# The sum of two quarters in the second product: made by an accumulating DMA that GpSimd issues instead of a VectorE addition

## The chip, the cores and the metric

The kernel runs on one core of one Trainium2 chip. The metric is the device time of one execution in microseconds (us), lower is better. The core has five engines that run side by side and wait for each other through semaphores: TensorE (PE, matrix products), VectorE (DVE), ScalarE (ACT), GpSimd (POOL) and SyncE (SP, which here only issues transfers), and 16 DMA engines that carry out the transfers.

## The reference

A banded attention (each query sees itself and the 63 keys before it) over 8 batches, 8 heads, 576 positions and head size 64 gives a matrix of 4608 tokens by 512 features. Two dense layers follow, with a leaky slope of its own for each hidden feature between them:

```
attn = softmax(mask(q @ k.T / 8)) @ v          # per batch and head, window 64
x = attn as (4608, 512)
h = x @ w_in                                    # (4608, 2048)
g = maximum(h, 0) + alpha * minimum(h, 0)       # alpha: one value per hidden feature
out = g @ w_out                                 # (4608, 512)
```

All data are fp32.

## The kernel before

**What is computed where.** The 4608 tokens are cut into nine blocks of 512 tokens (`n` from 0 to 8). The first product, with the attention ahead of it, takes some 490 us; its results `g` are stored to HBM in quarters of 128 by 512 values (`hidden`, line L840). The second product, `second(n)`, then reads them back. Each block is taken in four steps of hidden features, so that there are 36 **units**, `u = 4 n + d`. A unit is one step of a Strassen-Winograd scheme: the block's `g` is split in four quarters A11, A12, A21 and A22 (tiles `g_0`, `g_1`, `g_2`, `g_3` of one set; the numbers after them are instance numbers), four sums and differences of them are formed, and seven products instead of eight are made.

**The work of a unit**, in names of the program and lines of the profile:

- `gf`: four transfers bring the quarters from HBM into the set of the unit (SP queue, L927). There are four sets (`SETS`), so a set is used again four units later.
- `z3`: `diff = A11 - A21`; `z1`: `A21 = A21 + A22`, written over A21; `z2`: `A11 = A21 - A11`, with the new A21; `z4`: `A12 = A12 - A11`. All four are VectorE instructions on 128 by 512 values (L934). `z1` can't overwrite A21 before `z3` has read it, and `z2` needs the result of `z1`.
- `parts`, seven times: the values that a product needs are split in a high part `yh` (a cast on ScalarE, L939) and a rest `yl` (a subtraction on VectorE, L940). Such a pair is called a form here. The pairs lie in a ring of ten slots; a slot is filled again when TensorE has used it.
- `O.u.i`: the product of a form, twelve matmuls (L967: `wh,yh`, `wl,yh`, `wh,yl`).
- After the fourth unit of a block the accumulated banks are put together (one copy on ScalarE, L984, seven additions on VectorE, L975) and stored (L981).

GpSimd has no part in this stage but the end of the conversion of the weights of the second product (`wh`, `wl`, L393 a cast and L390 a subtraction), which it shares with ScalarE.

**What sets the order.** Every piece of work is an `Op` with its engine, a planned duration and what it reads and writes. `Program.order` plays the whole program through with these planned durations before the kernel is built, and so fixes the order of the instructions of every engine. On the chip each engine runs its instructions in this order: where one must wait, all behind it on that engine wait too. For a transfer the planner counts the issue (`0.5`), a `service` time on the DMA engines and a landing time:

```
self.done = min(busy + LAGS[e] for e, (busy, _) in ways.items()) + (service + LANDING if service else 0.0)
```

Of the kernel before, what the change touches and what calls it, by code (L numbers as in the profile page):

```python
# [14 lines left out]
ALU = mybir.AluOpType  # L15
# [236 lines left out]
def banded_attention_then_prelu_ffn(  # L252
# [11 lines left out]
    nc = tc.nc  # L264
# [76 lines left out]
    def halves_of(*bs):  # L341
        return [f"bank.{b}.{i}" for b in bs for i in range(2)]
# [3 lines left out]
    def add(name, engine, busy, emit, *args, **kw):  # L346
        p.add(name, {engine: (busy, emit)}, *args, **kw)
# [52 lines left out]
    def w_keys_of(x, slot, halves=range(2)):  # L400
        return [f"w{x}.{slot}.{i}" for i in halves]

    raw_at = [0]

    def chunk(name, c, f, second, start=0.0):
        r = raw_at[0] % (2 if second else RAWS)
        ulps, k_ulps = ulp_ring[raw_at[0] % 2], f"e.ulps.{raw_at[0] % 2}"
# [187 lines left out]
    def value(t, i, by=V_BANK):  # L595
        av = [bank_of(b).rearrange("p (i a) q -> p i a q", i=2)[:, i] for b in by]
        pt, at = turned[t % 2].rearrange("p a h u b q -> p a h (u b q)"), 2 * (t % KRING)
        for a in range(2):
            for block, to, from_ in ((1, slice(0, P), slice(W, 3 * W)), (0, slice(0, W), slice(0, W)),
                                     (2, slice(W, P), slice(3 * W, 4 * W))):  # L600
                for h in range(2):
                    for x in range(2):
                        r, hs = slice(x * W, (x + 1) * W), slice(h * D, (h + 1) * D)
                        nc.tensor.matmul(av[x][hs, a, to], vring[r, a, at + block, hs], pt[r, a, h, from_],  # L604
                                         start=block == 1, stop=block == 2)
# [162 lines left out]
    def begin_of(n, f=0):  # L768
        return BEGIN + (CELL * min(n, N0) + CELL2 * max(n - N0, 0)) * NF + (CELL if n < N0 else CELL2) * f
# [97 lines left out]
    def new_slot():  # L867

        at = ring["at"]
        ring["at"] += 1  # L870
        return at % SLOTS, SHIFTS[at]

    def y_of(kept, x, shift):
        return kept[x][:, 16 * shift:16 * shift + 512] if 4 <= x < 8 else kept[x]

    def slot_of_form(k):

        d, at = divmod(k, 7)
        return (3 * d, 3 * d + 1, 3 * d + 2, KEPT + 2 * d, KEPT + 2 * d + 1, KEPT + 2 * d + 8, KEPT + 2 * d + 9)[at]
# [34 lines left out]
    def y_keys(x):  # L914
        return [f"yh.{x}"], [f"yl.{x}"]

    def second(n):
# [4 lines left out]
        for d in range(DUOS):  # L922
            u = n * DUOS + d
            s = u % SETS
            base = begin_of(NB) + 4.0 + u * UNIT
            for q in range(4):
                add(f"gf.{u}.{q}", "SP", 0.5, lambda s=s, q=q, d=d: nc.sync.dma_start(g_of[s][q].rearrange("p (j t) -> p j t", j=2), hidden[n][d][:, q]),  # L927
                    ["left" if s else "right", *(f"far.g.{n}.{d}.{q}.{j}" for j in range(2))], [f"g.{s}.{q}"], service=0.9, earliest=base - 45)

            def cell(q, s=s):  # L930
                return lambda: g_of[s][q]

            def both(name, to, a, b, op, reads, writes):
                add(name, "DVE", 0.61, lambda: nc.vector.tensor_tensor(out=to(), in0=a(), in1=b(), op=op), reads, writes, paired=True)  # L934

            def parts(i, value, ks):
                x, (hi, lo) = slot_of[u, i] = new_slot()
                his, los = y_keys(x)
                add(f"ys.{u}.{i}.h", "ACT", 0.54, lambda: nc.scalar.copy(y_of(y_hi, x, hi), value()), [*ks, "right"], his)  # L939
                add(f"ys.{u}.{i}.l", "DVE", 0.61, lambda: nc.vector.tensor_tensor(out=y_of(y_lo, x, lo), in0=value(), in1=y_of(y_hi, x, hi).bitcast(F32), op=ALU.subtract),  # L940
                    [*ks, *his], los, paired=True)

            a11, a12, a21, a22 = (cell(q) for q in range(4))
            k11, k12, k21, k22 = ([f"g.{s}.{q}"] for q in range(4))
            d_ = lambda: diffs[0]
            parts(1, a11, k11)
            parts(2, a12, k12)
            both(f"z3.{u}", d_, a11, a21, ALU.subtract, [*k11, *k21], ["diff"])
            both(f"z1.{u}", a21, a21, a22, ALU.add, k22, k21)
            both(f"z2.{u}", a11, a21, a11, ALU.subtract, k21, k11)  # L950
            parts(6, a11, k11)
            parts(7, d_, ["diff"])
            parts(5, a21, k21)
            both(f"z4.{u}", a12, a12, a11, ALU.subtract, k11, k12)
            parts(3, a12, k12)
            parts(4, a22, k22)
            for at, i in enumerate(ORDER):
                (x, (hi, lo)), bank = slot_of[u, i], acc[i]

                k = 7 * d + at  # L960

                def emit(k=slot_of_form(k), x=x, bank=bank, d=d, hi=hi, lo=lo):
                    done = 0
                    for part, w in ((y_of(y_hi, x, hi), w_hi), (y_of(y_hi, x, hi), w_lo), (y_of(y_lo, x, lo), w_hi)):
                        for j in range(2):
                            for h in range(2):
                                nc.tensor.matmul(banks[bank][:, h * EH:(h + 1) * EH], part[:, j * HW + h * P:j * HW + (h + 1) * P],  # L967
                                                 w[k][:, j * EH:(j + 1) * EH], start=d == 0 and not done,
                                                 stop=d == DUOS - 1 and done == 11, skip_group_check=True)
                                done += 1  # L970

                add(f"O.{u}.{i}", "PE", STEP, emit, [*w_keys_of("h", slot_of_form(k)), *w_keys_of("l", slot_of_form(k)), *y_keys(x)[0], *y_keys(x)[1]], halves_of(bank), key=base + at * STEP)
# [70 lines left out]
    for n in range(NB):  # L1043
        second(n)
# [49 lines left out]
```

## Time and profile before

| | |
|---|---|
| median of 3 runs | 835.05 us |
| the 3 runs | 833.03 to 836.2 us |
| the profiled execution, its own time | 834.97 us |
| its span, first to last instruction | 833.2 us |
| busy: PE, DVE, ACT, POOL | 821.7, 704.3, 517.6, 386.7 us |
| granted TensorE clock, mean over the span | 1.000 of full speed |

The span is what the trace covers; the profiled execution's own time is 1.8 us longer. A busy TensorE is one with a matmul in it. The view by windows gives the same busy times for a stretch, the timeline gives single instructions with the idle time of the engine before them and what ended it.

### The profile page before, as it was taken

What the parts mean: (1) busy time and instruction counts of PE and PEld (TensorE: products, weight loads), DVE (VectorE), ACT (ScalarE), POOL (GpSimd) and SP (SyncE); (2) the same over time, 40 slices, a digit from 0 to 9 for tenths busy, and PEclk for the clock granted to TensorE, in tenths of its full rate; (3) what the DMA queues carried; (4) which work ended last, traced back from release to release, by engine and by line L of the source; (5) the groups of instructions that cost most, each with busy time, mean ns of one, the idle gap of its engine ahead of it and who ended that gap; (6) DMA issues with size and microseconds to landing.
All of it is one profiled execution on the core that took longest, in us unless ns stands there. A gap on an engine that the chain in (4) does not pass through costs nothing.

```text
span 833.2 us, 23747 instructions
## 1 busy us (share of the span) xinstructions
PE 821.7 (99%) x8974; PEld 791.4 (95%) x8974; DVE 704.3 (85%) x1821; ACT 517.6 (62%) x1382; POOL 386.7 (46%) x368
## 2 busy tenths in 40 slices
PE   9999999999999999999999999999999999999998
PEld 8988888999999999999999999999999999999997
DVE  4889798999998999989865868998888897979883
ACT  6887756788776687786965666444444444444441
POOL 5899999998276471948656977000000000000000
PEclk9999999999999999999999999999999999999999
DMA  8886455546557655777555896545353544535301
GB/s 253 274 254 220 148 172 159 165 145 217 188 177 241 211 197 174 247 262 236 185 212 168 285 297 241 175 140 177 100 174 121 156 124 139 165 103 172 95 26 51
DMA packets 108882, 150.97 MB, mean 181 GB/s; under 512 B 10464, under 2 KB 69856, under 8 KB 108768
## 3 DMA queue, kind: packets, MB, share of 16 engines
q1 hardware_dynamic: 106416, 149.19, 55.4%
q8 instruction: 70, 1.15, 0.6%
q10 hardware_dynamic: 2352, 0.27, 0.2%
q14 instruction: 44, 0.36, 0.1%
HBM read 94.90 MB, written 54.53 MB: 179 GB/s over the span
## 4 chain that ended last, share of the span: by engine, by line
PE 53%; DVE 4%; ACT 1%; issue 1%; DMA 1%; POOL 1%; SPq 0%; POOLq 0%; DVEq 0%; ACTq 0%
PE bank L967 41%; PE bank L823 11%; DVE cell L838 1%; DVE bank L844 1%; DVE w L557 1%; DMA q<-qT 1%; DVE pt L583 1%; ACT cell L837 1%; PE bank L588 0%; PE bank L604 0%; ACT w L564 0%; DVE pt L581 0%; PE bank L548 0%; DMA wo<-delta 0%; ACT r L851 0%
## 5 line engine op out<-in xcount | busy, mean ns | idle before, releaser
L939 ACT CAST yh<-g 128x512 fp32r<-128x512 f32 x216 | 132.8, 622 | 128.9 <-PE bank L967 85.6
L940 DVE TENSOR_TENSOR yl<-g,yh 128x512 fp32r<-128x512 f32 x216 | 149.3, 699 | 22.1 <-ACT yh L939 21.2
L967 PE MATMUL bank<-wh,yl 128*128 128x256 f32 x1008 | 155.8, 277 | 0.0
L967 PE MATMUL bank<-wl,yh 128*128 128x256 f32 x1008 | 155.8, 277 | 0.0
L967 PE MATMUL bank<-wh,yh 128*128 128x256 f32 x1008 | 155.7, 276 | 0.0
L967 PEld LDWEIGHTS bank<-wh,yh 128*128 128x128 f32 x1008 | 133.4, 188 | 0.0
L967 PEld LDWEIGHTS bank<-wl,yh 128*128 128x128 f32 x1008 | 133.3, 188 | 0.0
L967 PEld LDWEIGHTS bank<-wh,yl 128*128 128x128 f32 x1008 | 133.3, 188 | 0.0
L564 ACT ACTIVATE w<-w,nm 128x128 f32<-128x128 f32 x288 | 112.9, 398 | 26.0 <-DVE nm L557 26.0
L823 PE MATMUL bank<-xh,wh 128*128 128x256 f32 x560 | 113.1, 283 | 4.1 <-DVE bank L844 3.5
L838 DVE SCALAR_TENSOR_TENSOR cell<-bank,alphas,cell 128x256 f32<-128x256 f32 x224 | 96.1, 477 | 21.8 <-ACT cell L837 20.1
L837 ACT ACTIVATE cell<-bank,alphas 128x256 f32<-128x256 f32 x224 | 91.8, 476 | 35.1 <-PE bank L823 19.4
L573 POOL TENSOR_TENSOR w<-w,rc 128x512 f32<-128x512 f32 x72 | 76.9, 1086 | 78.5 <-DVE rc L569 30.7
L823 PE MATMUL bank<-xh,wl 128*128 128x256 f32 x560 | 109.7, 277 | 0.0
L823 PE MATMUL bank<-xl,wh 128*128 128x256 f32 x560 | 109.5, 277 | 0.0
L823 PEld LDWEIGHTS bank<-xh,wh 128*128 128x128 f32 x560 | 84.6, 188 | 8.3 <-DVE bank L844 4.9
L823 PEld LDWEIGHTS bank<-xh,wl 128*128 128x128 f32 x560 | 84.7, 188 | 0.0
L823 PEld LDWEIGHTS bank<-xl,wh 128*128 128x128 f32 x560 | 84.7, 188 | 0.0
L934 DVE TENSOR_TENSOR g<-g,g 128x512 f32<-128x512 f32 x108 | 75.6, 700 | 1.4
L557 DVE CUSTOM_DVE_ANT_0 w<-bank,masks 128x128 f32<-128x128 f32 x288 | 64.6, 284 | 10.2 <-PE bank L548 9.9
L844 DVE TENSOR_TENSOR bank<-bank,r 128x512 f32<-128x512 f32 x84 | 58.1, 692 | 17.2 <-PE bank L823 10.7
L564 ACT ACTIVATION_READ_ACCUMULATOR w<-w,nm 128x1 f32 x288 | 56.1, 195 | 0.0
(98 smaller groups left out, 1493.6 us busy)
## 6 DMA issues: line engine op xcount, KB each, us to landing
g<-g SPq DMA_DIRECT2D x144, 256.0 KB, 4.1
g<-cell SPq DMA_DIRECT2D x141, 256.0 KB, 3.3
out<-cell SPq DMA_DIRECT2D x36, 256.0 KB, 2.3
q<-qT SPq DMA_DIRECT2D x35, 256.0 KB, 4.9
raw<-w_out SPq DMA_DIRECT2D x16, 512.0 KB, 5.2
wl<-wo SPq DMA_DIRECT2D x28, 256.0 KB, 4.6
v<-vN SPq DMA_DIRECT2D x18, 384.0 KB, 5.4
k<-kT SPq DMA_DIRECT2D x17, 384.0 KB, 4.9
```

Of the source, the lines that this page charges most:

```text
L557: nc.vector.tensor_tensor_reduce(out=of_head(weights[t % 2], g), in0=bank_of(score_banks(t, g // NP)[x])[:, e].rearrange("p (b k) -> p b k ...
L564: nc.scalar.activation(w, w, AF.Exp, scale=-1.0, bias=least[t % 2][:, g:g + 1], accum_out=sums[:, t % 2, g, 0:1])
L573: nc.gpsimd.tensor_tensor(out=w, in0=w, in1=rc.unsqueeze(1).unsqueeze(3).broadcast_to(list(w.shape)), op=ALU.mult)
L583: nc.vector.transpose(to[:, :, j ^ 1], w[:, x, j, :, j ^ 1])
L823: nc.tensor.matmul(h, at_place(w, place)[:, c * P:(c + 1) * P], v[:, c], start=new and j == 0 and not done, stop=j == 1 and done == 5, ski ...
L837: add(f"sl.{n}.{d}.{m}.{x}.{j}", "ACT", 0.36, lambda h=h, g=g, f=f: nc.scalar.activation(g, h, AF.Copy, scale=slope[:, f:f + 1]), ["signs" ...
L838: add(f"la.{n}.{d}.{m}.{x}.{j}", "DVE", 0.43, lambda h=h, g=g, f=f: nc.vector.scalar_tensor_tensor(out=g, in0=h, scalar=sign[:, f:f + 1], ...
L844: add(f"{name}.{n}.{d}", "DVE", 0.6, lambda: nc.vector.tensor_tensor(out=to, in0=a, in1=b, op=ALU.add), reads, k_to)
L934: add(name, "DVE", 0.61, lambda: nc.vector.tensor_tensor(out=to(), in0=a(), in1=b(), op=op), reads, writes, paired=True)
L939: add(f"ys.{u}.{i}.h", "ACT", 0.54, lambda: nc.scalar.copy(y_of(y_hi, x, hi), value()), [*ks, "right"], his)
L940: add(f"ys.{u}.{i}.l", "DVE", 0.61, lambda: nc.vector.tensor_tensor(out=y_of(y_lo, x, lo), in0=value(), in1=y_of(y_hi, x, hi).bitcast(F32) ...
L967: nc.tensor.matmul(banks[bank][:, h * EH:(h + 1) * EH], part[:, j * HW + h * P:j * HW + (h + 1) * P], w[k][:, j * EH:(j + 1) * EH], start= ...
```

## The change

One line of `second`: the VectorE addition `z1` becomes a transfer from A22 to A21 within SBUF that adds what it brings to what lies there. It is issued by GpSimd and planned with 0.5 us of GpSimd, a service of 1.8 us and the landing time.

```
             parts(1, a11, k11)
             parts(2, a12, k12)
             both(f"z3.{u}", d_, a11, a21, ALU.subtract, [*k11, *k21], ["diff"])
-            both(f"z1.{u}", a21, a21, a22, ALU.add, k22, k21)
+            add(f"z1.{u}", "POOL", 0.5, lambda a21=a21, a22=a22: nc.gpsimd.dma_start(a21(), a22(), accum_op=ALU.add), k22, k21, service=1.8)
             both(f"z2.{u}", a11, a21, a11, ALU.subtract, k21, k11)
             parts(6, a11, k11)
             parts(7, d_, ["diff"])
```

Since the planner plays the program anew, the order of other instructions moves too, from about the last block of the first product on. Three places follow.

**VectorE, a unit in the middle of the second product** (unit 14; `diff` is z3, the row that writes `g_0` is z2, the one that writes `g_1` is z4, each `yl` is the rest of a form). Before:

```order
L934 TENSOR_TENSOR diff<-g_0_7380,g_2_7382 128x512
L940 TENSOR_TENSOR yl_6683<-g_1_7377,yh_6682 128x512
L934 TENSOR_TENSOR g_2_7382<-g_2_7382,g_3_7383 128x512
L940 TENSOR_TENSOR yl_6685<-g_3_7379,yh_6684 128x512
L975 TENSOR_TENSOR cell_124<-bank_169,r_7388 128x512
L940 TENSOR_TENSOR yl_6688<-g_0_7380,yh_6687 128x512
L934 TENSOR_TENSOR g_0_7380<-g_2_7382,g_0_7380 128x512
L940 TENSOR_TENSOR yl_6690<-g_1_7381,yh_6689 128x512
L934 TENSOR_TENSOR g_1_7381<-g_1_7381,g_0_7380 128x512
```

And of the changed kernel, the same unit:

```order
L934 TENSOR_TENSOR diff<-g_0_7377,g_2_7379 128x512
L940 TENSOR_TENSOR yl_6683<-g_1_7374,yh_6682 128x512
L940 TENSOR_TENSOR yl_6685<-g_3_7376,yh_6684 128x512
L940 TENSOR_TENSOR yl_6688<-g_0_7377,yh_6687 128x512
L940 TENSOR_TENSOR yl_6690<-g_1_7378,yh_6689 128x512
L934 TENSOR_TENSOR g_0_7377<-g_2_7379,g_0_7377 128x512
L934 TENSOR_TENSOR g_1_7378<-g_1_7378,g_0_7377 128x512
L940 TENSOR_TENSOR yl_6672<-diff,yh_6671 128x512
L940 TENSOR_TENSOR yl_6670<-g_0_7377,yh_6669 128x512
```

The addition into `g_2` is gone, and four `yl` stand between z3 and z2, which now waits for the transfer. Counted in the same way, the instructions between z3 and z2 are 10 to 16 in units 0 to 9, 5 and 4 in units 10 and 11, and from unit 12 on 4, 8, 4 and 5 in every round of four units.

**VectorE, where the second product has just begun to run alone** (units 1 to 3: their `diff` rows, and what is behind them, to the first z2). Before, the first nine instructions:

```order
L940 TENSOR_TENSOR yl_6685<-g_0_7376,yh_6684 128x512
L934 TENSOR_TENSOR diff<-g_0_7376,g_2_7378 128x512
L934 TENSOR_TENSOR g_2_7378<-g_2_7378,g_3_7379 128x512
L940 TENSOR_TENSOR yl_6676<-g_3_7379,yh_6675 128x512
L934 TENSOR_TENSOR g_0_7376<-g_2_7378,g_0_7376 128x512
L940 TENSOR_TENSOR yl_6688<-g_1_7377,yh_6687 128x512
L940 TENSOR_TENSOR yl_6670<-diff,yh_6669 128x512
L940 TENSOR_TENSOR yl_6690<-g_0_7376,yh_6689 128x512
L934 TENSOR_TENSOR g_1_7377<-g_1_7377,g_0_7376 128x512
```

Of the changed kernel:

```order
L934 TENSOR_TENSOR diff<-g_0_7373,g_2_7375 128x512
L940 TENSOR_TENSOR yl_6676<-g_3_7376,yh_6675 128x512
L940 TENSOR_TENSOR yl_6670<-diff,yh_6669 128x512
L940 TENSOR_TENSOR yl_6688<-g_1_7374,yh_6687 128x512
L940 TENSOR_TENSOR yl_6679<-g_0_7377,yh_6678 128x512
L934 TENSOR_TENSOR diff<-g_0_7377,g_2_7379 128x512
L940 TENSOR_TENSOR yl_6685<-diff,yh_6684 128x512
L940 TENSOR_TENSOR yl_6681<-g_1_7378,yh_6680 128x512
L940 TENSOR_TENSOR yl_6670<-g_3_7380,yh_6669 128x512
L934 TENSOR_TENSOR diff<-g_0_7381,g_2_7383 128x512
L940 TENSOR_TENSOR yl_6679<-diff,yh_6678 128x512
L934 TENSOR_TENSOR g_0_7373<-g_2_7375,g_0_7373 128x512
```

Forms that need no `z1` (of units 1, 2 and 3) are drawn ahead, so that ten instructions stand between z3 and z2 of unit 1. TensorE's products are drawn ahead in the same way.

**GpSimd, the end of the weights' conversion.** Before, the last instructions of its program are these:

```order
L390 TENSOR_TENSOR wl_100<-wl_100,wh_72 128x512
L393 CAST wh_73<-wl_101 128x512
L390 TENSOR_TENSOR wl_101<-wl_101,wh_73 128x512
L390 TENSOR_TENSOR wl_102<-wl_102,wh_74 128x512
L390 TENSOR_TENSOR wl_117<-wl_117,wh_89 128x512
L390 TENSOR_TENSOR wl_118<-wl_118,wh_90 128x512
```

Of the changed kernel:

```order
L390 TENSOR_TENSOR wl_100<-wl_100,wh_72 128x512
L949 DMA g_2_7375<-g_3_7376 128x512
L949 DMA g_2_7379<-g_3_7380 128x512
L949 DMA g_2_7383<-g_3_7384 128x512
L393 CAST wh_73<-wl_101 128x512
L390 TENSOR_TENSOR wl_101<-wl_101,wh_73 128x512
L390 TENSOR_TENSOR wl_102<-wl_102,wh_74 128x512
```

The issues of the transfers of units 1, 2 and 3 stand ahead of the last four pieces of weights; that of unit 0 stands further ahead, behind the first one; those of units 4 to 35 follow at the end with nothing between them.

## Rows read from the trace of the kernel before

**Rows 1.** Page: busy us of each engine (share of the span) and instructions.

```profile
PE 821.7 (99%) x8974; PEld 791.4 (95%) x8974; DVE 704.3 (85%) x1821; ACT 517.6 (62%) x1382; POOL 386.7 (46%) x368
```

**Rows 2.** Windows: from:to, length, busy us (instructions) by engine, clock, DMA share, GB/s.

```profile
440.00:460.00 20.00, 19.10 (x165) 18.70 (x164) 13.06 (x26) 12.16 (x27) 13.71 (x12) 1.00 0.58 194
460.00:489.00 29.00, 29.00 (x250) 28.83 (x249) 21.43 (x37) 20.60 (x45) 28.92 (x23) 1.00 0.87 279
489.00:829.00 340.00, 340.00 (x2991) 339.93 (x2989) 286.42 (x451) 158.09 (x262) 21.38 (x10) 1.00 0.45 140
```

**Rows 3.** Chain that ended last, in order of time: start, us, what.

```profile
489.30 339.84 PE bank L967 x2988
829.16 0.69 DVE cell L975
```

**Rows 4.** Timeline of TensorE: start, us, operation, count [idle before <-releaser].

```profile
451.36 0.51 PE L823 MATMUL bank<-sh,wh 128*128 128x256 f32 x2 [0.85 <-DVE bank L844]
...
497.14 0.63 PE L967 MATMUL bank<-wh,yl 128*128 128x256 f32 x4
```

**Rows 5.** Timeline of VectorE, 456 to 516 us.

```profile
456.28 0.68 DVE L934 TENSOR_TENSOR diff<-g,g 128x512 f32<-128x512 f32 x1
...
458.26 0.68 DVE L934 TENSOR_TENSOR g<-g,g 128x512 f32<-128x512 f32 x1
...
493.77 1.78 DVE L934 TENSOR_TENSOR diff<-g,g 128x512 f32<-128x512 f32 x1
495.58 0.69 DVE L934 TENSOR_TENSOR g<-g,g 128x512 f32<-128x512 f32 x1
496.19 0.68 DVE L940 TENSOR_TENSOR yl<-g,yh 128x512 fp32r<-128x512 f32 x1
...
505.23 2.48 DVE L940 TENSOR_TENSOR yl<-g,yh 128x512 fp32r<-128x512 f32 x4
...
510.05 0.68 DVE L934 TENSOR_TENSOR g<-g,g 128x512 f32<-128x512 f32 x1
514.00 1.63 DVE L940 TENSOR_TENSOR yl<-diff,yh 128x512 fp32r<-128x512 f32 x1 [3.27 <-ACT yh L939]
```

**Rows 6.** Timeline of ScalarE, one cast of the second product.

```profile
620.68 0.62 ACT L939 CAST yh<-diff 128x512 fp32r<-128x512 f32 x1 [0.75 <-PE bank L967]
```

**Rows 7.** Timeline of VectorE, 621 to 623 us.

```profile
621.34 0.69 DVE L940 TENSOR_TENSOR yl<-diff,yh 128x512 fp32r<-128x512 f32 x1 [0.67 <-ACT yh L939]
622.06 0.69 DVE L934 TENSOR_TENSOR diff<-g,g 128x512 f32<-128x512 f32 x1
```

**Rows 8.** Timeline of GpSimd, 453 to 516 us.

```profile
453.05 1.29 POOL L390 TENSOR_TENSOR wl<-wl,wh 128x512 fp32r<-128x512 f32 x1
458.16 1.25 POOL L393 CAST wh<-wl 128x512 fp32r<-128x512 f32 x1 [3.83 <-DMA wl<-wo]
...
461.85 0.61 POOL L393 CAST wh<-wl 128x512 fp32r<-128x512 f32 x1
...
488.20 6.80 POOL L390 TENSOR_TENSOR wl<-wl,wh 128x512 fp32r<-128x512 f32 x5
501.33 9.87 POOL L393 CAST wh<-wl 128x512 fp32r<-128x512 f32 x1 [6.33 <-DMA wl<-wo]
511.28 5.51 POOL L390 TENSOR_TENSOR wl<-wl,wh 128x512 fp32r<-128x512 f32 x4
```

**Rows 9.** DMA issues, 520 to 820 us: count, KB each, median us to landing.

```profile
g<-g SPq DMA_DIRECT2D x113, 256.0 KB, 3.8
out<-cell SPq DMA_DIRECT2D x32, 256.0 KB, 2.4
```

**Rows 10.** Page: the queue with most bytes (packets, MB, share of 16 engines), two larger transfers.

```profile
q1 hardware_dynamic: 106416, 149.19, 55.4%
...
raw<-w_out SPq DMA_DIRECT2D x16, 512.0 KB, 5.2
...
stage<-w_in SPq DMA_DIRECT2D x5, 512.0 KB, 5.9
```

More of the change, by code (lines that the diff above doesn't have):

```diff
@@ L948, in second @@
             both(f"z3.{u}", d_, a11, a21, ALU.subtract, [*k11, *k21], ["diff"])
-            both(f"z1.{u}", a21, a21, a22, ALU.add, k22, k21)
+            add(f"z1.{u}", "POOL", 0.5, lambda a21=a21, a22=a22: nc.gpsimd.dma_start(a21(), a22(), accum_op=ALU.add), k22, k21, service=1.8)
             both(f"z2.{u}", a11, a21, a11, ALU.subtract, k21, k11)
```

## The prediction

> **What bounds the kernel now.** I read the busy time of each engine first, then windows, then the chain that ended last, then timelines. The page gives TensorE 821.7 us of a span of 833.2 [rows 1]. The windows say where that matters: from 460 to 829 us TensorE is busy without a gap [rows 2], and the chain ends with one piece of 339.84 us in which TensorE waits for nobody, behind which only one VectorE addition and a store are left [rows 3]. So in the second product TensorE alone sets the time. One matmul there takes 339.84 / 2988 = 0.1137 us, a form of twelve 1.365, a unit of seven forms 9.55, a round of four units (one block) 38.2.
>
> VectorE is the one to watch all the same: 286.42 of 340 us are busy [rows 2]. Its instructions of 128 by 512 can follow each other every (2.48 - 0.68) / 3 = 0.60 us [rows 5]. A round has 4 x 11 of them (four sums, seven rests) and 7 additions at its end: 51, or 30.6 of 38.2 us.
>
> How far VectorE is ahead decides what a delay costs. The cast at 620.68 began when TensorE freed a slot of the ring [rows 6], and its rest was done at 622.03 [rows 7]. Nine other forms are used before that slot's turn comes, 9 x 1.365 = 12.3 us after it was freed, so the form was complete 10.9 us before its use. At the start of the stage this lead isn't there yet: the rest written at 496.19 ended at 496.87 and the matmul that reads it began at 497.14, 0.27 us later [rows 4, 5]. From 496 to 511 us VectorE works without a pause, builds up the lead, and has its first idle time of 3.27 us at 514 [rows 5].
>
> **What the change removes.** 36 instructions of 0.60 us, 21.7 us of VectorE. That is worth nothing on the path, since TensorE has no gap from 460 us on. Its last idle time ahead of that is 0.85 us at 451.36 [rows 4], and the first instruction that goes is the addition at 458.26, behind it [rows 5]. Gain: 0. What it gives is spare time: a round of VectorE falls to 47 instructions, 28.2 us, and 10.0 us of the round are free.
>
> **What it adds.** A transfer of 256 KB per unit, on which z2 waits. No row shows an accumulating transfer or one issued by GpSimd, so I bound the time L from the end of z3 to the moment when z2 may start. For the issue on GpSimd: between its shortest and its usual work on 128 by 512 values, 0.61 and 1.29 us [rows 8]. For issue to landing of plain 256 KB: 2.4 us for stores, 3.8 for loads in the same stretch [rows 9]. For the second thing to be read, the old A21: the busiest queue moved 149.19 MB in 55.4% of the span [rows 10], 323 GB/s, so 0.8 us for another 256 KB. The sum is 3.8 to 5.9 us. I take the middle, 4.9, since nothing draws it to either end. The outer bounds are 2.4 (a store, and nothing for issue and addition) and 1.29 + 5.9 = 7.2, with the slowest 512 KB load [rows 10].
>
> *In a steady round* (units 12 to 35, six rounds) 4, 8, 4 and 5 instructions stand between z3 and z2. If VectorE is behind, they take 0.60 us each, and since an instruction ends 0.08 us after the next has begun, its wait per unit is L + 0.08 - 0.60 x (instructions between). Over a round that is 4 L - 12.3 us. At 4.9 it is 7.3 us, less than the 10.0 that are free: the lead stays, TensorE sees nothing. Break-even is L = 5.6. Beyond it a round loses 4 L - 22.3 us; six rounds first eat the lead of 10.9 us, and the rest is lost time. So 0.5% (4.2 us) is lost at L = 6.2, and 28 us at the bound of 7.2. What is late then: z2 holds up all rests behind it on VectorE, and TensorE waits for them.
>
> *At the start* (units 1 to 3) the thin place gets better: without the addition at 495.58 the rest used at 497.14 is done 0.6 us sooner. z3 of unit 1 ended at 495.55 [rows 5] and GpSimd is free at 495.0 [rows 8], so the first transfer lands at about 500.5. z2 of unit 1 has ten instructions ahead of it, and one of them, the rest of unit 2's A22, needs a slot that TensorE frees two forms after the one ending at about 497.6 [rows 4], at 500.3. With its cast and rest behind that (1.35 us as in rows 6 and 7) and three more instructions, z2 starts at about 503, 2.5 us after the landing. The transfers of units 2 and 3 begin at about 498 and 502 and have ten and twelve instructions too. Cost: 0. Units 4 to 9 have 11 to 16 instructions, 6.6 us at least, and units 10 and 11 sit on a lead already built.
>
> *On GpSimd's queue* the issue of unit 0 falls behind z3 at 456.28 [rows 5], into the 3.83 us in which GpSimd waited for weights [rows 8]. Those of units 1 to 3 stand ahead of the last four weight pieces, so the cast that began at 501.33 can't begin before z3 of unit 3, at about 503. Its weights are then some 2 us later than before. I count 0, since TensorE didn't wait for them, and keep the case as a rival. From there on GpSimd has only these issues, one per 9.55 us. SP's queue loses and gains nothing; the new 256 KB per unit meet DMA engines that are 45% busy [rows 2].
>
> **Sum.** 834.97 us for the profiled execution (span 833.2 and 1.8 around it), less 0, plus 0: **835.0 us**. The execution stands 0.1 us below the median of the three runs, 835.05; these lie 0.4% apart, so about 0.5%, 4 us, is what a measurement of this kernel can tell from no change.
>
> **A rule that speaks against the change.** In these rows GpSimd can be shut out: the cast of 128 by 512 that takes 0.61 us at 461.85 took 9.87 us from 501.33 [rows 8], exactly while VectorE ran additions and subtractions of two SBUF inputs without a pause, and it ended at 511.20, half a us after VectorE stopped [rows 5]. The Trainium skill (SBUF — State Buffer, section "SBUF: two separate sides") says that a transfer issued by GpSimd has its descriptors written by GpSimd's cores, and that these are shut out while VectorE holds the port pair that both share. By that the sum would be the second rival's 882 us. The same page (section "Who interferes with whom") says that a VectorE instruction with two SBUF inputs shuts out only what reads SBUF on GpSimd, while writing descriptors needs the write side. By that the sum stays 835.0. The cast reads SBUF, so the row agrees with both, and no row here shows a descriptor being written.
>
> **The rivals.**
> 1. *The transfer lands late* (slower). Place: z2 of units 12 to 35. It decides from L = 6.2 us. Price as above: 846 us at 6.5, 863 at 7.2. For it: loads in this stretch come in groups of up to four, with a median of 3.8 us against 2.4 for the stores between them [rows 9], and nothing says how fast the addition runs. Against it: even 5.9, all three terms at their upper ends but the large load, isn't enough.
> 2. *GpSimd is shut out while VectorE works*, as its cast was, so that L only starts when VectorE has stopped at z2 (slower). Then every z2 waits the full 4.9: 19.6 us a round against 10.0, 9.6 x 6 - 10.9 = 47 us, so 882. Against it: with a full lead VectorE pauses before most rests, 0.67 us at 621.34 [rows 7], and lets GpSimd in.
> 3. *The queue of GpSimd holds up the last weights* (slower). The cast starts 2 us late, and if the issues ahead of it are shut out like the cast was, up to 9.9 us. Price 2 to 10 us: about 840.
> 4. *VectorE's relief shows after all* (faster). All idle time of TensorE from 440 us on to the end of its work is 0.9 us [rows 2], so 834.1 at best, which would pass for no change. To be faster by 4 us, matmuls would have to get shorter, for which no row speaks.
>
> **How the numbers follow.** No change, transfer hidden: 0.63, own range 832 to 839 (the spread of the runs). Rival 1: 0.22, rival 2: 0.07, rival 3: 0.05, faster for a reason I don't see: 0.03. The range from 832 to 863 us takes in rival 3 and rival 1 up to its bound and leaves out the shut-out queue, landings over 7.2 us and the gain, together some 0.15. Faster by over 0.5%: 0.03, within 0.5%: 0.63, slower: 0.34.
>
> **What will show it.** Right: TensorE without a gap from about 460 us to its end, VectorE some 22 us less busy, 36 issues on GpSimd, idle time of VectorE ahead of z2 with the transfer as releaser, at most some 2 us a time, and rests still about 10 us ahead of their matmuls at the end. Wrong: waits of 3 us and more at most z2, a lead that shrinks from round to round, TensorE waiting for `yl`; or TensorE waiting for `wh` or `wl` near 515 us; or time lost before 460 us, where the order has moved too and I count nothing.

## The result and the profile after

The changed kernel takes 840.64 us (median of 18 runs, lowest 835.38) against 834.94 for the kernel before: a ratio of 1.0059, 95% interval 1.0037 to 1.0081. It is slower by a little over half a per cent, where no change was forecast. Two of the 18 runs, at 909.54 and 1166.59 us, were run at a granted clock of 0.85 and 0.66 and are left out of the ratio.

The profiled execution (836.51 us, span 834.8) is one of the faster ones. First the page's busy times, then windows (columns as in [rows 2]):

```profile
PE 822.4 (99%) x8974; PEld 792.0 (95%) x8974; DVE 678.5 (81%) x1785; ACT 506.8 (61%) x1385; POOL 406.0 (49%) x401
```

```profile
440.00:460.00 20.00, 19.14 (x168) 18.95 (x167) 13.49 (x26) 12.70 (x29) 13.21 (x12) 1.00 0.63 213
460.00:489.00 29.00, 28.79 (x244) 28.39 (x244) 19.55 (x36) 20.30 (x45) 24.09 (x19) 1.00 0.84 272
489.00:520.00 31.00, 29.75 (x254) 29.55 (x254) 26.80 (x32) 18.64 (x35) 16.99 (x14) 1.00 0.90 280
520.00:829.00 309.00, 309.00 (x2726) 309.00 (x2725) 236.52 (x384) 127.23 (x230) 27.83 (x32) 1.00 0.58 156
```

VectorE is 25.8 us less busy [rows 1] and has 36 instructions fewer. TensorE, without a gap from 460 us in [rows 2], now stands still for 0.21 us before 489 and 1.25 us before 520. The last piece of the chain that ended last starts at 498.23, not at 489.30 [rows 3]:

```profile
498.23 332.26 PE bank L967 x2920
830.51 0.69 DVE cell L975
```

What ends that gap is a rest of VectorE (the `yl` of a form). The timeline of the changed kernel around it (start, length, engine and operation, in brackets the idle time ahead of it and what ended that):

```profile
490.44 7.19 POOL L390 TENSOR_TENSOR wl<-wl,wh 128x512 fp32r<-128x512 f32 x5 [1.30 <-ACT wh L393]
...
492.99 1.80 DVE L940 TENSOR_TENSOR yl<-g,yh 128x512 fp32r<-128x512 f32 x1 [2.23 <-ACT yh L939]
...
494.72 1.77 DVE L934 TENSOR_TENSOR diff<-g,g 128x512 f32<-128x512 f32 x1
496.41 1.76 DVE L940 TENSOR_TENSOR yl<-g,yh 128x512 fp32r<-128x512 f32 x1
...
498.23 0.74 PE L967 MATMUL bank<-wh,yl 128*128 128x256 f32 x4 [1.25 <-DVE yl L940]
```

GpSimd waits 1.30 us for a weight cast of ScalarE and works on its splits until 497.63; before, it was done at 495.0 [rows 8]. Beside it these three VectorE instructions take 1.76 to 1.80 us; such an instruction alone takes 0.68. Before, one of the instructions ahead of this rest was slow, and the rest ended at 496.87 [rows 5]; now three are, and it ends at 498.17. The addition that was removed from just this place had cost 0.60. Set against the kernel before, matmul by matmul, 1.5 us are lost with this gap. Some 0.7 us were lost ahead of it, between 467 and 486 us, where the gap of 0.21 us (at 468.73, behind a VectorE instruction of the first product) lies; what brought about this part is not settled.

The transfers, from the line that issues them (ns, min/median/max; then us from issue to landing), and, of the stretch from 610 to 763 us, four rounds, VectorE's waits in the changed kernel, those in the kernel before, and the window of the changed kernel:

```profile
L949 POOL DMA_DIRECT2D g<-g x36: 862/870/1019, 456.3 to 813.0; - x36
...
DMA to landing us min/median/max: 3.3/4.8/8.2
```

```profile
DVE g L934 <- DMA g<-g: 37.5, 12, 4.1
```

```profile
DVE yl L940 <- ACT yh L939: 21.2, 28, 1.6
```

```profile
610.00:763.00 153.00, 153.00 (x1352) 153.00 (x1352) 114.81 (x187) 62.52 (x116) 13.90 (x16) 1.00 0.59 158
```

In the kernel before, VectorE waited in this stretch 21.2 us, only for casts of ScalarE: it was ahead, and held back by free slots. Now it waits 37.5 us at z2, three times a round, and for nothing else. With the 114.81 us in which it is busy that makes 152.3 of 153 us: VectorE has no time to spare. One unit of it:

```profile
649.33 0.69 DVE L934 TENSOR_TENSOR diff<-g,g 128x512 f32<-128x512 f32 x1
649.93 2.50 DVE L940 TENSOR_TENSOR yl<-g,yh 128x512 fp32r<-128x512 f32 x4
650.66 0.89 POOL L949 DMA_DIRECT2D g<-g  x1 [8.15 <-DVE yl L940]
656.28 1.42 DVE L934 TENSOR_TENSOR g<-g,g 128x512 f32<-128x512 f32 x2 [3.86 <-DMA g<-g]
```

z3 ends at 650.02, the issue starts 0.64 us later, and z2 at 656.28, 0.09 us after the landing at 656.19: up to the landing L was 6.2 here.

**Where the time goes, execution by execution.** All kernels here have the same 8,974 matmuls, so the start of matmul 5,601 (at 443 us in the kernel before), of 6,401 (537 us) and of the last (829 us) can be set against that kernel's own. This splits the difference into three: ahead of 443 us, where executions differ by some 1 us either way and in one by 3; from there to 537 us, the *start* of the second product; and behind it, the *steady* part. Worked out in this way from each trace (us), beside the runs:

| kernel | profiled | to 443 | start | steady | median (runs) | ratio, 95% interval |
|---|---|---|---|---|---|---|
| changed | 836.51 | -1.0 | +2.4 | 0.0 | 840.64 (18) | 1.0059 [1.0037, 1.0081] |
| after_again | 840.33 | -0.1 | +2.4 | +2.9 | 841.80 (6) | 1.0074 [1.0046, 1.0102] |
| after_third | 842.54 | +1.0 | +2.1 | +4.3 | one run | |
| after_fourth | 845.06 | +1.3 | +2.2 | +6.3 | one run | |
| free_sum | 837.41 | -0.1 | +2.4 | 0.0 | 837.44 (12) | 1.0021 [1.0002, 1.0041] |
| plan_only | 838.08 | 0.0 | +3.0 | 0.0 | 838.15 (11) | 1.0048 [1.0027, 1.0068] |
| more_room | 838.07 | -1.1 | +4.4 | 0.0 | 839.07 (12) | 1.0041 [1.0024, 1.0057] |
| two_transfers | 839.60 | -0.5 | +2.0 | +3.3 | 842.56 (10) | 1.0073 [1.0050, 1.0096] |
| early_units | 836.83 | -0.3 | +1.9 | 0.0 | 836.96 (12) | 1.0015 [0.9993, 1.0037] |
| late_units | 835.82 | +0.6 | 0.0 | 0.0 | 835.22 (12) | 0.9994 [0.9970, 1.0018] |
| plain_copy | 836.70 | -0.2 | +1.7 | 0.0 | 836.88 (10) | 1.0009 [0.9988, 1.0031] |
| from_four | 842.25 | +0.1 | +0.1 | +6.7 | 842.25 (5) | 1.0089 [1.0072, 1.0106] |
| room_late | 836.27 | -1.0 | +2.2 | 0.0 | 836.99 (12) | 1.0034 [1.0019, 1.0049] |
| casts_back | 838.53 | -1.0 | +3.8 | 0.0 | 839.47 (9) | 1.0060 [1.0036, 1.0084] |
| hold_once | 834.59 | -0.2 | -0.4 | +0.2 | 835.50 (10) | 1.0007 [0.9982, 1.0033] |
| from_four_room | 831.75 | -3.1 | 0.0 | 0.0 | 834.63 (12) | 0.9996 [0.9980, 1.0012] |
| late_room | 834.48 | -0.5 | +0.2 | 0.0 | 834.50 (12) | 1.0004 [0.9986, 1.0022] |

The changed kernel loses 2.1 to 2.4 us at the start in all four profiled executions, and 0 to 6.3 in the steady part. The sum of both fits its median. The kernels were run on different chips; each ratio is to the kernel before on the same chip, whose median was 834.7 to 835.0 us each time.

### The profile page after: what moved, and what is told of

Same layout as the page of the kernel before. It is cut to its first block, busy times and chain, and to the rows that moved or that the text cites. A ratio compares the mean times of both kernels' runs of the same rounds, so it can differ in the third digit from the quotient of the medians.

```text
span 834.8 us, 23843 instructions
## 1 busy us (share of the span) xinstructions
PE 822.4 (99%) x8974; PEld 792.0 (95%) x8974; DVE 678.5 (81%) x1785; ACT 506.8 (61%) x1385; POOL 406.0 (49%) x401
## 4 chain that ended last, share of the span: by engine, by line
PE 52%; DVE 5%; ACT 3%; issue 1%; POOL 1%; DMA 0%; DVEq 0%; POOLq 0%; ACTq 0%
PE bank L967 40%; PE bank L823 10%; DVE cell L838 1%; ACT w L564 1%; ACT cell L837 1%; DVE bank L844 1%; DVE pt L583 1%; PE bank L588 0%; PE bank L604 0%; DVE w L557 0%; DVE yl L940 0%; DVE pt L581 0%; ACT wh L393 0%; ACT r L851 0%; PE bank L548 0%
## 5 line engine op out<-in xcount | busy, mean ns | idle before, releaser
L939 ACT CAST yh<-g 128x512 fp32r<-128x512 f32 x216 | 122.1, 620 | 164.8 <-DVE g L934 140.5
L949 POOL DMA_DIRECT2D g<-g x36 | 31.5, 874 | 275.0 <-DVE yl L940 176.6
L940 DVE TENSOR_TENSOR yl<-g,yh 128x512 fp32r<-128x512 f32 x216 | 146.5, 714 | 5.3 <-ACT yh L939 4.8
L934 DVE TENSOR_TENSOR g<-g,g 128x512 f32<-128x512 f32 x72 | 52.5, 729 | 62.4 <-DMA g<-g 61.7
```

The lines of the kernel that those rows point to most:

```text
L949: add(f"z1.{u}", "POOL", 0.5, lambda a21=a21, a22=a22: nc.gpsimd.dma_start(a21(), a22(), accum_op=ALU.add), k22, k21, service=1.8)
```

## The experiments

The first eight kernels were chosen before this split was seen. Theory A in their expectations is that z2's waits in the steady rounds cost most of the time and VectorE and GpSimd get in each other's way at the start, for up to 1.5 us. Rival B is that the transfers cost by themselves (traffic and issue), rival C that the moved order alone costs.

**after_again**: the changed kernel, unchanged.

> The changed kernel itself, beside the three others. Theory A (z2 waits for a transfer that lands 4 to 7 us after z3, so that in the steady rounds VectorE needs 38.7 us where TensorE needs 38.2, and the lead shrinks; another 1.5 us go at the start of the second product, where VectorE and GpSimd get in each other's way) expects 837 to 841 us, 1.003 to 1.008 of the kernel before. Rival B (the transfers cost time by themselves, through their traffic on the DMA engines and their issue on GpSimd, not through a wait) and rival C (only the moved order costs) expect the same here.

840.33 us in the profile, 841.80 in the median. It lost 2.9 us in the steady part, which the first profile did not show.

**free_sum**: the transfer without anybody waiting for it, from unit 4 on. (The diffs of this section are cut to the lines that matter; the new tile `spares[0]` is left out.)

```diff
-nc.gpsimd.dma_start(a21(), a22(), accum_op=ALU.add)
+nc.gpsimd.dma_start(spares[0] if u > 3 else a21(), a22(), accum_op=ALU.add)
```

> The order of the changed kernel, but from unit 4 on the transfer adds A22 to a tile that nobody reads, so that z2 waits for nothing; left out is the sum itself, z2 and the fifth form use the plain A21. Theory A: no wait at z2 from unit 4 on, the lead of the rests stays at 9 to 12 us to the end, and only the 1.5 us of the start remain: 836 to 837 us, ratio 1.001 to 1.003. Rival B: all the transfers are still there, so 838 to 841. Rival C: 838 to 841, since the order is the same.

Start +2.4, steady 0.0: with nobody waiting for them, as many transfers and issues cost nothing behind 537 us. They came at other moments, though: nothing ties these transfers to z3, and GpSimd issued them as soon as A22 was there and the one before had landed. What is left is the start; 837.44 us is a little above theory A's 836 to 837.

**plan_only**: the changed order with VectorE's addition where the issue stood.

```diff
-nc.gpsimd.dma_start(a21(), a22(), accum_op=ALU.add)
+nc.vector.tensor_tensor(out=a21(), in0=a21(), in1=a22(), op=ALU.add)
```

> The order of the changed kernel, with the sum made by a VectorE addition at the place where the transfer was issued: no transfer, no wait on one. Theory A: the start still loses up to 1.5 us, the steady rounds nothing: 835 to 837 us, ratio 1.000 to 1.003. Rival B: 835, ratio 1.000. Rival C: 838 to 841, since the order is the changed one.

There is no transfer in it, and the start costs 3.0 us, the steady part nothing. So the start's loss comes from the order, not from transfers; it is twice what theory A gave it, and 838.15 us lies in rival C's range, but rival C does not explain the steady losses of the changed kernel.

**more_room**: `service=1.8` became `service=3.8`, so that the planner puts mostly 14 to 20 instructions between z3 and z2.

> The changed kernel with the planner's service time of the transfer at 3.8 us instead of 1.8, so that 14 to 20 instructions instead of 4 to 8 stand between z3 and z2 in the steady rounds, which is 8 us and more. Theory A: no waits for the transfer from unit 12 on, the lead stays, and 1 to 2 us of the start remain: 835.5 to 837.5 us, ratio 1.001 to 1.003. Rival B: 838 to 841 as the changed kernel, since the transfers are as many. Rival C: can't say, since the order moves again.

Steady 0.0, but the planner moved the start again, to +4.4, and 839.07 us is above the range expected: a gain and a loss that the time alone doesn't show apart.

**two_transfers**: one more transfer, in the program ahead of the real one, from unit 4 on.

```diff
+if u > 3:
+    nc.gpsimd.dma_start(spares[0], a22(), accum_op=ALU.add)
 nc.gpsimd.dma_start(a21(), a22(), accum_op=ALU.add)
```

> The order of the changed kernel; from unit 4 on GpSimd issues a second transfer of the same size ahead of the real one, into a tile that nobody reads. Theory A: the real one lands later by its issue, 0.9 us, and by up to 1.5 us of DMA time, so 1 to 2.4 us; the last 24 units lose 4 times that a round: 6 x 4 x (1 to 2.4) = 24 to 58 us over the changed kernel, 860 to 900 us, and TensorE waits for rests in every round. Rival B: twice the cost of the transfers, 844 to 848. Rival C: 838 to 841.

The steep rise did not come. The page's rows of the two (KB each, median us from issue to landing):

```profile
g<-g POOLq DMA_DIRECT2D x36, 256.0 KB, 5.2
...
spare<-g POOLq DMA_DIRECT2D x32, 256.0 KB, 7.0
```

But on the chip the extra transfer was not where the expectation put it. It waits for A22 alone, not for z3, so GpSimd issued it right behind the real one of the unit before (L953 is the extra one, L954 the real one):

```profile
621.50 0.87 POOL L954 DMA_DIRECT2D g<-g  x1 [7.20 <-DVE yl L942]
622.11 1.15 POOL L953 DMA_DIRECT2D spare<-g  x1
630.23 0.86 POOL L954 DMA_DIRECT2D g<-g  x1 [6.96 <-DVE yl L942]
```

The extra one of 622.11 landed at 629.26, ahead of the next real issue, and so in every unit from 9 on. What ran side by side was a real transfer and an extra one issued some 0.6 us behind its start: the real one then landed after 5.2 us in place of 4.8. So twice the traffic hardly lengthens the wait, and the account of theory A for a transfer directly ahead of the real one was not put to the test.

**late_units** and **early_units**: VectorE's addition for `u < 10` and the transfer for the rest, and the other way round, each planned anew.

> The transfer from unit 10 on alone, VectorE's addition in units 0 to 9, planned anew. Theory A: the start is that of the kernel before, and the steady rounds are those of the changed kernel, whose lead of some 11 us at unit 12 shrinks by 0.5 to 1 us a round and in the worse executions runs out: 835 to 839 us, ratio 1.000 to 1.005. Rival B: 26 of 36 transfers, 0.7 of the cost: 838 to 839. Rival C: 835.

> The transfer in units 0 to 9 alone, VectorE's addition from unit 10 on. Theory A: the start loses its 1.5 us, nothing else: 836 to 837 us, ratio 1.001 to 1.003, and a lead of 9 to 12 us to the end. Rival B: 10 of 36 transfers, 0.3 of the cost: 836 to 837. Rival C: 838 to 841.

The late transfers alone cost nothing in start or steady part, the early ones alone only +1.9 at the start. The losses do not simply add up: in late_units VectorE's additions that free TensorE's banks were 7.9 us ahead at 600 us and still 2.2 in the last round, so the lead did not run out; in the changed kernel it began at 5.3 (see below).

**plain_copy**: the same transfer without `accum_op`, so that z2 reads A22 in place of the sum.

> The order of the changed kernel, with a plain transfer in place of the accumulating one; A21 is overwritten by A22, the sum is left out. This measures what the addition costs the transfer. Theory A: the DMA engines need 0.8 us instead of 1.5 per transfer, it lands some 0.7 us sooner, 4 x 0.7 = 2.8 us a round are more than the 0.5 that are missing: 836 to 837 us, the lead stays. Rival B: half the traffic, 837 to 838. Rival C: 838 to 841.

Steady 0.0. It lands sooner (page row; the accumulating one has 4.8):

```profile
g<-g POOLq DMA_DIRECT2D x36, 256.0 KB, 4.1
```

Of the 0.7 us, 0.33 lie in the issue, 0.54 us in place of 0.87. With that the same lead is 7.5 us at 600 us and recovers to 8.25; the accumulation is what brings VectorE to its limit.

**from_four**: VectorE's addition for `u < 4`, transfers behind it. From here on the expectations set the account of two places (start and steady part) against its rivals.

> VectorE adds A22 to A21 for units 0 to 3, the transfer for units 4 to 35, planned anew; GpSimd's and ScalarE's instructions ahead of 520 us are then those of the kernel before. Theory of two steps (a moved order at the start costs 2 to 2.5 us; the waits at z2 eat the lead of the additions that free TensorE's banks, and only where this reaches zero is more lost): no loss at the start, that lead begins near 8 us at 600 us and ends near 2, TensorE has no gap and its matmuls keep 0.113 us; 834.5 to 836.5. Rival (the waits at z2 cost by themselves, whatever the start was): 838 to 841, with gaps of TensorE behind 700 us.

The start was as expected (+0.1), the steady part was not: 6.7 us lost, the most of all. The account had put the small lead down to the start, and this part of it falls. With less room from the planner (4 instructions between z3 and z2 of units 8, 10 and 11, where the changed kernel has 11, 5 and 4), the lead was 2.5 us at 600 us and gone at 641. Of the 6.7 us, 4.6 are hold-ups of TensorE and most of the rest slower matmuls (last section).

**room_late**: the changed kernel with `service=1.8 if u < 10 else 3.8`.

> The changed kernel; only the planner's service time of the transfer is 3.8 in place of 1.8 from unit 10 on, so that it puts 14 to 20 instructions between z3 and z2 there. Theory of two steps: the start costs 2.4 us as in the changed kernel, the lead of the additions that free the banks stays over 4 us, the matmuls keep 0.113 us to the end; 837 to 838. Rival (the transfers cost by their traffic or by their issue): 840 to 842 as in the changed kernel.

Start +2.2, steady 0.0, 836.99 us: the rival is out. The same transfers with 8 to 12 instructions between z3 and z2 in most units (not the 14 to 20 expected), where there were 4 to 8, cost nothing, and the lead stays over 7 us to the end.

**casts_back**: as room_late, with five weight casts tied to the engine of the kernel before.

```diff
-        o = Op(name, ways, key, ...
+        o = Op(name, {PINNED[name]: ways[PINNED[name]]} if name in PINNED else ways, key, ...
```

> As the one with more room from unit 10 on, and the five weight casts that the planner moved between GpSimd and ScalarE are tied to the engine that they had in the kernel before. If these casts are what costs at the start (GpSimd ends its splits 2.6 us later and slows VectorE's additions on the path from 0.7 to 1.8 us), the gap of TensorE near 498 us shrinks from 1.4 to under 0.4 us; 835 to 836.2. If it is the rest of the moved order or the first transfers, the gap stays; 837 to 838.

The start got worse (+3.8), and 839.47 us lies above both ranges. The gap near 498 us shrank from 1.25 to 0.69 us, where under 0.4 was expected; GpSimd still waits for ScalarE and ends late, and a second gap came:

```profile
490.74 1.30 POOL L390 TENSOR_TENSOR wl<-wl,wh 128x512 fp32r<-128x512 f32 x1 [1.27 <-ACT wh L393]
...
492.68 6.38 POOL L390 TENSOR_TENSOR wl<-wl,wh 128x512 fp32r<-128x512 f32 x4
...
497.97 0.74 PE L967 MATMUL bank<-wh,yl 128*128 128x256 f32 x4 [0.69 <-DVE yl L940]
...
511.23 0.74 PE L967 MATMUL bank<-wh,yl 128*128 128x256 f32 x4 [1.47 <-DVE yl L940]
```

That these five casts alone are the cause is refuted.

**hold_once**: the kernel before, with 16 further additions of VectorE into a tile that nobody reads, once, in unit 14.

> The kernel before, with 16 further additions into a tile that nobody reads, behind the addition of unit 14 alone: VectorE falls 9.6 us back once, and TensorE waits about 1 to 2 us once, near 605 us. If a short hold-up leaves TensorE at the slower of two matmul rates (0.118 for 0.113 us) for a long while: 840 to 847, and the rows behind the gap show it. If only the hold-up itself counts: 836 to 837.5, and 0.113 us right behind it.

The 16 additions took VectorE 11.6 us, not 9.6, and TensorE was held up once, by 0.23 us, at 618.57, right behind a rest that ended at 618.52; 835.50 us, and the matmuls kept 0.113 us behind it. That every hold-up leaves TensorE slower is refuted; and the lead of the rests, 10.9 us in the prediction, takes a single delay of about its own size.

**from_four_room** and **late_room**: as from_four and late_units, with `service=3.8` for all transfers.

> VectorE's addition for units 0 to 3, the transfer for units 4 to 35 with the planner's service time at 3.8, so that 7 to 19 instructions stand between z3 and z2. Account of two places (moved order at the start, z2's waits that use up VectorE's spare time): no loss at either, TensorE without a gap from 460 us on, leads of 7 us and more, 834.3 to 836. Rival (the transfers cost by their traffic, issue or queue): 838 to 842 as with service 1.8.

> VectorE's addition for units 0 to 9, the transfer with service time 3.8 for units 10 to 35. Account of two places: no loss, 834.3 to 836, the same as the kernel before; VectorE some 15 us less busy, which buys nothing. Rival (VectorE's relief is worth something once its waits are gone): under 833.

Both lose nothing at either place. VectorE's waits of from_four_room between 610 and 763 us, and its windows:

```profile
DVE yl L940 <- ACT yh L939: 34.1, 24, 2.9
```

```profile
460.00:489.00 29.00, 29.00 (x251) 28.86 (x249) 20.94 (x36) 20.23 (x45) 29.00 (x24) 1.00 0.82 257
489.00:825.00 336.00, 336.00 (x2958) 336.00 (x2957) 261.16 (x415) 151.27 (x257) 46.22 (x39) 1.00 0.58 164
```

32 transfers, no wait for any of them, TensorE without a gap: 834.63 us, within the measurement of the kernel before (its 831.75 in the profile comes from the stretch ahead of 443 us). No version is faster than that kernel: VectorE's relief buys nothing.

**after_third** and **after_fourth**: the changed kernel, one execution each.

> The changed kernel once more. Account: 2.4 us lost at 495 to 515 us, and where the additions that free the banks come less than 0.2 us ahead of the matmul that needs the bank, a hold-up there and slower matmuls (0.118 us) behind it; 838 to 843. Rival (the extra of the longer executions lies elsewhere, ahead of 440 us or spread evenly): no hold-up at the banks, a drift over the whole span.

> The changed kernel once more, the same expectations as for the third look: the time over 837.5 and a hold-up at the banks come together or not at all.

Steady part +4.3 and +6.3, with hold-ups at the banks in both. The waits of TensorE behind 600 us in after_fourth (us, times, longest), and the longest of them in the timeline:

```profile
PE bank L967 <- ACT r L984: 2.1, 3, 1.4
PE bank L967 <- DVE cell L975: 0.8, 3, 0.3
```

```profile
793.05 0.86 POOL L949 DMA_DIRECT2D g<-g  x1 [8.20 <-DVE yl L940]
...
799.29 0.69 DVE L934 TENSOR_TENSOR g<-g,g 128x512 f32<-128x512 f32 x1 [4.48 <-DMA g<-g]
...
800.10 0.62 ACT L939 CAST yh<-g 128x512 fp32r<-128x512 f32 x1 [6.62 <-DVE g L934]
800.62 0.58 ACT L984 COPY r<-bank 128x512 f32<-128x512 f32 x1
...
801.25 0.74 PE L967 MATMUL bank<-wh,yh 128*128 128x256 f32 x4 [1.40 <-ACT r L984]
```

The whole steady mechanism can be followed here: the transfer lands late, z2 starts after a wait of 4.48 us, ScalarE's cast of z2's result comes behind it, and behind that cast in ScalarE's queue stands the copy that frees the first bank of the round. TensorE waits for it. The hold-ups themselves make up 0.2 us of the steady loss in after_again, 2.0 in after_third and 5.9 in after_fourth; the remaining 2.7, 2.3 and 0.4 us are matmuls at a slower rate (last section).

## Why the prediction was wrong

**The bound and the gain: right.** 36 additions gone, VectorE 25.8 us less busy, no time gained; in from_four_room and late_room, which lose nothing, neither. Rival 4 is out.

**L: the term that was mis-sized.** The prediction took 4.9 us, in bounds of 2.4 to 7.2, and break-even at 5.6. Over units 12 to 31 the four profiled executions of the changed kernel have a mean L, up to the landing, of 5.41, 5.44, 5.54 and 5.66 (z2 can start 0.09 us later), and steady losses of 0.0, 2.9, 4.3 and 6.3 us: in this order. Its parts: 0.65 us from z3's end to the start of the issue, which no term had; 0.87 for the issue (in the prediction's 0.61 to 1.29); and 2.4 us from there to landing where nothing else was under way, up to 5.9 where loads were. The 2.4 is as much as the median of plain stores, which is counted from the start of their issue [rows 9]. The waits of the changed kernel come to 9.0 to 10.6 us in each of the rounds from unit 12 to 31 (prediction: 7.3); free were 10.0 by the prediction, and 9.5 by the busy time between 610 and 763 us. So VectorE, with 21.7 us of work taken from it, had become as slow as TensorE. plain_copy shows the other side: 0.7 us less in each landing, and the lead recovers.

**The lead: the step that failed.** The prediction let six rounds eat a lead of 10.9 us, measured at a rest. But the thinnest lead is that of the instructions that free the banks at a round's end. The first VectorE addition there ended 8.25 us before TensorE needed its bank in the kernel before, in every round from 600 us on; in the changed kernel 5.3, 3.4, 2.8, 2.2, 2.0 and 0.7 us, round by round, and in after_fourth 4.6, 1.6, 0.1, 0.1, 0.1 and 0.1, where TensorE stands. The lead was at 5.3 when the steady rounds began; the waits of units 10 and 11 (3.4 and 3.1 us), which the prediction left out of its six rounds, had come before. "TensorE waits for them", said of the rests, was thus the second thing to be late; the banks came first. And the price of running out was not only the hold-ups: the slower matmuls behind them, which no term had, are over half of the steady loss in two of the three executions that lost time there, and their cause stays open.

**The start: a step counted at 0 that cost 2.1 to 2.4 us.** The prediction saw the thin place, and that the addition leaves it, and made it 0.6 us better. It did not ask what the planner's moves do to GpSimd there: its splits end 2.6 us later, and three of VectorE's instructions beside them take 1.77 us each (in plan_only too: splits to 498.52, slow instructions to 499.07). That goes with the 1.5 us at the gap, not with the 0.7 ahead of it. Of z2 and the transfers of units 1 to 3 it was right: z2 of units 1 to 9 waited for no transfer, although the first landed at 505.73 and not 500.5. plan_only shows that the order does it, and from_four, late_units, from_four_room and late_room that the loss goes where units 0 to 3 (or 0 to 9) keep the old order. Which of the moved instructions it hangs on is open: the five casts alone, as casts_back shows, are not it.

**Rival 2: out.** The issues took 0.86 to 1.02 us, the longest included, also while VectorE ran pairs of SBUF inputs without a pause; GpSimd was not shut out of them. The Trainium skill (SBUF — State Buffer, section "Who interferes with whom") says that such an instruction contends with what reads SBUF on GpSimd and not with what only writes it, and the trace agrees on both halves: 0.87 us for the issues, and 1.77 for 0.68 us on VectorE beside GpSimd's splits. The sentence in the section "SBUF: two separate sides" of that page of the Trainium skill, by which GpSimd can't write descriptors, is about a VectorE operation in a 2-port mode; the prediction stretched it to pairs of SBUF inputs, and for these the issues above do not bear it out.

**Rival 3: out.** The cast behind the issues of units 1 to 3 started at 504.75 and took 0.96 us in place of 9.87 [rows 8]; no profile of the changed kernel shows TensorE waiting for the last weights. **Rival 1**, the late landing, is nearest to what happened, at an L below its 6.2.

## What to carry to other kernels

Taking work from an engine that isn't the bound bought nothing here, but the latency that comes in its place counts against that engine's in-order queue: set the sum of the waits in a round against the free time of the round, and look for the thinnest lead among everything that stands behind the wait (here the freeing of a bank, on another engine than the one that waits). Room, not speed, was the cure: seven or more instructions between z3 and the use of the sum made 32 transfers free. Where a planner orders the work, a change of one operation's engine moves others at the thinnest place of the program; run the new order without the new operation to see what that alone costs.

## What the runs showed of the hardware that was not expected

TensorE's matmuls of 256 columns follow each other at one of two rates, at a granted clock of 1.00. Windows of after_again:

```profile
600.00:760.00 160.00, 160.00 (x1414) 160.00 (x1413) 118.81 (x194) 64.92 (x121) 13.90 (x16) 1.00 0.59 160
762.00:829.00 67.00, 67.00 (x570) 67.00 (x570) 49.53 (x81) 26.04 (x48) 5.24 (x6) 1.00 0.45 118
```

160 / 1414 is 0.113 us, 67 / 570 is 0.118. The change came with a hold-up of 0.2 us at a bank, at 762 us, and lasted to the end: of the 2.9 us lost there, some 2.7 are the slower matmuls. In from_four and after_fourth the rate changed at some hold-ups and changed back, at another hold-up or without one; in hold_once it did not change. The prediction had only priced the hold-ups themselves. What decides between the two rates is not settled.

An accumulating transfer of 256 KB inside SBUF took the 16 DMA engines 1.5 us of their time (6.6% of 834.8 us for 36), the plain copy of the same bytes 0.7 (2.9%); a second one issued 0.6 us behind its start delayed its landing by only 0.4 us. The queue of these transfers in the changed kernel and in plain_copy (packets, MB, share of the span of 16 engines):

```profile
q0 software_dynamic: 5184, 9.44, 6.6%
```

```profile
q0 software_dynamic: 2880, 9.44, 2.9%
```
